# Later v loads, free accumulator banks for the first block's scores, and single vector steps per slot in an attention + FFN kernel

## The chip, the cores and the metric

The kernel runs on one core of a Trainium2 chip. The metric is the device time of one execution in microseconds, smaller being better. The core has TensorE (PE; its weight loads are listed apart as PEld), VectorE (DVE), ScalarE (ACT), GpSimd (POOL) and SyncE (SP, which here only issues transfers). Each engine takes its instructions in program order.

## What is computed

For each of 4 batches, with a sequence of 3136, `d_model` 256, `d_qk` 64 and `d_ff` 1024:

```python
scores = (1.0 / S) * z @ z.T                 # S x S, symmetric
attn   = np.maximum(scores, 0.0) ** 2
x      = u * (attn @ v)
h      = np.maximum(x @ w_in, 0.0)
conv   = sum(conv_w[k] * shift(h, k - 1) for k in range(3))   # along the sequence
out    = (h / (1 + np.exp(-conv))) @ w_out
```

## The kernel before

**Tiles.** The sequence of a batch is cut into 7 blocks of 448 columns; 28 blocks in all. For each block the kernel walks over 25 row tiles of 128 rows; one row tile of one block is a *slot*, so there are 700 slots. To keep float32 accuracy every operand of a product is split into a high and a low part (`vh`/`vl`, `ah`/`al`, `gh`/`gl`, ...) and a product is three matmuls.

**Attention.** For a computed row tile `k`, `scores` runs two matmuls into an accumulator bank with the tag `s` (two such banks), `relu` (ACT) writes the scaled ReLU to SBUF tile `t`, `square` (DVE, L309) multiplies in place in the bank, `split_hi` (ACT, `ah`) and `split_lo` (DVE, `al`, recorded at the helper's L122) make the two parts, and `attend` runs six matmuls (L337 to L339) into the two `av` banks. `split_lo` is the last reader of the `s` bank. Because the scores are symmetric, a part of the row tiles of a block is not computed: `part` (GpSimd, L270) copies `t` to a tile `pl` (three buffers), `spill` (SP, L282) writes it to a scratch tensor `dq`, and a later block takes it back with `fetch` (SP, a transposing transfer, L290), `join` (GpSimd, L296, tile `tj`) and a Square on ACT (L301). In block q of a batch 0, 3, 7, 10, 14, 17 and 21 of the 25 row tiles come back that way.

**FFN.** The FFN of block b runs during the slots of block b+1, in eight steps f of 128 columns, which begin at the slots `FS`. `ffn_in` runs six matmuls (L370 to L372, twice) into a bank with the tag `ph` (two banks); ReLU to `hb` (ACT, L393), first tap (ACT, L402, in place in `ph`), two more taps (DVE, L407), Sigmoid (ACT, L414), the product with `hb` (DVE, L421), then `gh` (ACT) and `gl` (low part, L122), and ten slots after `ffn_in` the products `ffn_out` (L438 to L440). For blocks q of 0 to 2 the low part is on GpSimd: then the product goes to an SBUF tile `c` and the `ph` bank is free after it. For q of 3 to 6 it is on DVE: the product stays in the `ph` bank, which is free after `gl`.

**v.** `load_v` (SP, L168) brings two row tiles of v into a tile `vst` (three buffers); `prep_v` copies them to `vh` (ACT) and makes `vl` (GpSimd, L122). In block 0 this runs just ahead of the use; for the next batches it runs in the last block of the batch before and in the first of its own.

**Order.** The order is written by hand. In slot k the engines receive: class PRE; `split_hi`, `split_lo` of row tile k+2; class MID; `relu`, `square` of k+3; class VEC; class POST; `fetch` of k+9, `join` of k+5, `part` of k+2, `spill` of k+1; class PE0; `attend` of k; `scores` of k+4; class PE1. The FFN's steps are put into these classes by `at(slot, class, ...)`. The number after `C_` is the class (0 PRE to 5 PE1), the other constants are slots after the step's first one.

Of the kernel before, what the change touches and what calls it, by code (L numbers as in the profile page):

```python
# [8 lines left out]
F32 = mybir.dt.float32  # L9
# [19 lines left out]
LA, LT, LS = 4, 3, 2  # L29
# [1 line left out]


FS = [2, 5, 8, 11, 15, 18, 21, 24]
RELU, TAP, ST1, ST2, SIG, GATE, GHI, GLO, OUT0, OUT1 = 1, 1, 2, 2, 3, 4, 5, 6, 10, 11
EVAC = 12
XS = 1

C_GATE, C_ST1, C_ST2, C_G, C_SIG, C_HI, C_LO = 0, 2, 2, 2, 3, 3, 2
C_TAP, C_XS, C_EV, C_V = 3, 3, 3, 5

QV = 3


WS = [0, 8, 11, 17, 15, 21, 27, 22, 29, 34, 36, 38, 40, 45, 48, 53]
# [14 lines left out]
def kernel(  # L59
# [15 lines left out]
    P = 128  # L75
    NB = 448
    QB = S // NB
    NJ = (S + P - 1) // P
# [11 lines left out]
    ps = ctx.enter_context(tc.tile_pool(name="ps", bufs=1, space=bass.MemoryType.PSUM))  # L90
# [14 lines left out]
    def at_slot(k):  # L105
        blk, i = divmod(k, NJ)
        return blk, *ent[blk % QB][i]
# [139 lines left out]
    def scores(k):  # L247
        blk, j, tr = at_slot(k)
        if tr:
            return  # L250
        s = ps.tile([P, 512], F32, tag="s", name="s", bufs=2)
        w = slice(j * P, (j + 1) * P)
        nc.tensor.matmul(s[:, :NB], lhsT=zhh[:, w], rhs=zq[blk], start=True, stop=False)  # L253
        nc.tensor.matmul(s[:, :NB], lhsT=zll[:, w], rhs=zq[blk], start=False, stop=True)  # L254
        sc[k] = s
# [108 lines left out]
    ph, hb, cc, gg, po = {}, {}, {}, {}, {}  # L364
# [30 lines left out]
            nc.gpsimd.tensor_copy(halo[:, f], t[:, NB : NB + 2])  # L395

    def ffn_tap(blk, f):
        e = width(blk)  # L400
        cc[blk, f] = c = ph.pop((blk, f))[:, :e]
        nc.scalar.mul(c, hb[blk, f][:, :e], cw[:, f, 0:1])  # L402
# [68 lines left out]
    V, A, G = nc.vector, nc.scalar, nc.gpsimd  # L471
# [4 lines left out]
    PRE, MID, VEC, POST, PE0, PE1 = range(6)  # L476

    def at(slot, cls, fn, *args):
        ev[slot][cls].append((fn, args))


    for q in range(2, QB):
        s = (7 * q) // 2 - LA - 2
# [1 line left out]
        at(s, POST, prep_z, q)  # L485
    at(-3, POST, prep_z, 1)
    for j in range(2, NJ, 2):
        at(max(j - 9, -LA), POST, load_v, 0, j)
        at(j - 3, C_V, prep_v, j, A)


    for b in range(1, B):
        k0 = (b * QB - 1) * NJ
        for q in range(QB):
            s = k0 - (QB - 2 - q) * NJ + (12 if q % 2 == 0 else 4)
            if q == QB - 2:
                s = k0 + 6
            elif q == QB - 1:
                s = k0 + NJ + 6
            at(s - 4, POST, load_z, b, q)  # L500
            at(s, POST, prep_z, q)
        last = {j: i for i, (j, _) in enumerate(ent[QB - 1])}
        for j in range(0, NJ, 2):
            s = k0 + max(last[j] + 2, last.get(j + 1, 0) + 2, V0 + V1 * j // NJ)
            at(s - 6, POST, load_v, b, j)
            at(s, C_V, prep_v, j, A)
    for blk in range(1, NBLK):
        at(blk * NJ - LA - 2, VEC, queries, blk)
# [2 lines left out]
    for i, (_, what, f) in enumerate(sorted(need)):  # L511
        s = WS[i]
# [8 lines left out]
    for blk in range(NBLK - 1):  # L521
        k0 = (blk + 1) * NJ
        at(k0, C_GATE, gate_x, blk, G)
        at(k0 + XS, C_XS, split_x, blk, (G, G))
        for f in range(FC):
            s = k0 + FS[f]
            at(s, POST, ffn_halo, blk, f)
            at(s, PE1, ffn_in, blk, f)
            at(s + RELU, C_TAP, ffn_relu, blk, f)
            at(s + TAP, C_TAP, ffn_tap, blk, f)  # L530
            at(s + ST1, C_ST1, ffn_conv, blk, f, 1)
            at(s + ST2, C_ST2, ffn_conv, blk, f, 2)
            at(s + SIG, C_SIG, ffn_sig, blk, f)
            lo = V if (blk + 1) % QB >= QV else G
            at(s + GATE, C_G, ffn_gate, blk, f, lo)
            at(s + GHI, C_HI, ffn_hi, blk, f, A)
            at(s + (GLO if lo is V else GHI), C_LO if lo is V else PE1, ffn_lo, blk, f, lo)
            at(s + OUT0, PE0, ffn_out, blk, f, 0)
            at(s + OUT1, PE0, ffn_out, blk, f, 1)
        at(s + EVAC, C_EV, evac, blk)  # L540
        at(s + EVAC + 2, POST, store, blk)
# [28 lines left out]
    with tc.manual_schedule():  # L570
# [12 lines left out]
        for k in range(-LA, max(ev) + 1):  # L583
            e = ev[k]
            run(e[PRE])
            if 0 <= k + LS < NS:
                split_hi(k + LS)
                split_lo(k + LS)
            run(e[MID])
            if 0 <= k + LT < NS:  # L590
                relu(k + LT)
                square(k + LT)
            run(e[VEC])
            run(e[POST])
            if 0 <= k + LD < NS:
                fetch(k + LD)
            if 0 <= k + LJ < NS:
                join(k + LJ)
            if 0 <= k + LP < NS:
                part(k + LP)  # L600
            if 0 <= k + LX < NS:
                spill(k + LX)
            run(e[PE0])
            if 0 <= k < NS:
                attend(k)
            if k + LA < NS:
                scores(k + LA)
            run(e[PE1])
# [41 lines left out]
```

## Time and profile before

| | us |
|---|---|
| median of 3 runs | 1699.93 (1699.38 to 1700.0) |
| the profiled execution | 1699.81 |
| its span, first to last instruction | 1697.7 |
| mean granted TensorE clock | 0.992 |

The profiled execution lies 2.1 us above its span and 0.1 us below the median of the runs. Matmuls are pipelined: each is recorded with about 0.37 us, while in a stretch without stalls one starts every 0.2 us or so. The busy share of TensorE therefore hides short stalls, and the number of matmuls in a stretch, against its length, says more.

### The profile page before, as it was taken

The numbers are of one execution on the slowest core, as the hardware profiler recorded it, in microseconds if no ns is written. First come the engines' busy times: TensorE is split into PE (matmuls) and PEld (weight loads), VectorE is DVE, ScalarE is ACT, GpSimd is POOL, SyncE is SP. The second block draws the span as 40 slices with busy tenths as digits, with TensorE's granted clock in tenths as the row PEclk, the third lists the DMA queues.
The fourth block names the chain that finished last, engine by engine and source line by source line (L and its number), as shares of the span: only waits on it lengthen the run. The fifth ranks groups of instructions, "written<-read, shape, count | busy, mean of one in ns | idle before, by whom it ended". The sixth has DMA issues, their size and how long they took to land.

```text
span 1697.7 us, 24837 instructions
## 1 busy us (share of the span) xinstructions
PE 1615.3 (95%) x7656; PEld 1433.9 (84%) x7656; DVE 1215.1 (72%) x2080; ACT 1277.1 (75%) x2562; POOL 982.5 (58%) x1345
## 2 busy tenths in 40 slices
PE   6689999999999999999999999999999999999998
PEld 5578888888889888888888988889889898888886
DVE  5788667776777767677767766777677776677766
ACT  5577777778777777777887777777877777777785
POOL 5767555556566654546575665555657566445551
PEclk9899999999999999999999999999999999999999
DMA  5543444456324434445543343454634334444540
GB/s 154 154 116 103 111 108 90 106 119 148 107 88 125 109 87 123 99 108 112 124 140 84 107 120 98 102 108 106 133 100 139 93 92 107 103 104 98 109 93 22
DMA packets 384485, 184.59 MB, mean 109 GB/s; under 512 B 275296, under 2 KB 383328, under 8 KB 384352
## 3 DMA queue, kind: packets, MB, share of 16 engines
q1 hardware_dynamic: 384208, 182.77, 43.5%
q8 instruction: 60, 0.98, 0.2%
q14 instruction: 73, 0.60, 0.1%
q10 hardware_dynamic: 144, 0.23, 0.0%
HBM read 36.59 MB, written 80.28 MB: 69 GB/s over the span
## 4 chain that ended last, share of the span: by engine, by line
PE 72%; DVE 13%; issue 6%; ACT 6%; POOL 1%; DMA 1%; SPq 0%; POOLq 0%; DVEq 0%; ACTq 0%
PE av L337 11%; PE av L338 11%; PE av L339 11%; PE ph L370 6%; PE ph L372 5%; PE ph L371 5%; PE s L253 5%; PE o L440 4%; PE o L438 4%; PE o L439 4%; PE s L254 4%; DVE al L122 3%; DVE s L309 3%; DVE ph L407 3%; ACT t L304 2%
## 5 line engine op out<-in xcount | busy, mean ns | idle before, releaser
L122 DVE TENSOR_TENSOR al<-s,ah 128x448 fp32r<-128x448 f32 x672 | 418.1, 622 | 369.1 <-ACT ah L316 198.4
L337 PE MATMUL av<-ah,vl 128*128 128x448 f32 x1344 | 496.0, 369 | 10.2 <-POOL vl L122 7.8
L338 PE MATMUL av<-ah,vh 128*128 128x448 f32 x1344 | 494.6, 368 | 0.0
L339 PE MATMUL av<-al,vh 128*128 128x448 f32 x1344 | 493.1, 367 | 0.0
L296 POOL COPY tj<-tp 128x896 uint16<-128x896 uint16 x288 | 348.4, 1214 | 1.9 <-DMA tp<-dq 1.5
L304 ACT ACTIVATE t<-s 128x448 f32<-128x448 f32 x412 | 225.4, 547 | 129.9 <-PE s L254 104.7
L407 DVE SCALAR_TENSOR_TENSOR ph<-hb,cw,ph 128x448 f32<-128x448 f32 (+1 forms) x448 | 306.8, 685 | 13.1 <-ACT ph L402 5.4
L309 DVE TENSOR_TENSOR s<-s,t 128x448 f32<-128x448 f32 x412 | 258.7, 628 | 78.2 <-ACT t L304 77.2
L270 POOL COPY pl<-t 128x896 uint16<-128x896 uint16 x312 | 290.7, 940 | 14.8 <-DMA dq<-pl 13.8
L395 POOL COPY halo<-hb 128x2 f32<-128x2 f32 x192 | 37.0, 192 | 451.1 <-ACT hb L393 450.7
L316 ACT CAST ah<-s 128x448 fp32r<-128x448 f32 x412 | 219.2, 532 | 98.0 <-DVE s L309 97.0
L337 PEld LDWEIGHTS av<-ah,vl 128*128 128x128 f32 x1344 | 254.6, 189 | 36.4 <-POOL vl L122 10.4
L339 PEld LDWEIGHTS av<-al,vh 128*128 128x128 f32 x1344 | 254.4, 189 | 21.3
L338 PEld LDWEIGHTS av<-ah,vh 128*128 128x128 f32 x1344 | 254.8, 190 | 20.4
L393 ACT ACTIVATE hb<-ph 128x448 f32<-128x448 f32 x224 | 122.6, 547 | 118.8 <-PE ph L372 117.2
L253 PE MATMUL s<-zq,zhh 128*128 128x448 f32 x412 | 163.6, 397 | 39.8 <-DVE al L122 31.0
L370 PE MATMUL ph<-xh,wih 128*128 128x448 f32 x448 | 171.9, 384 | 28.1 <-DVE gl L122 26.0
L314 ACT ACTIVATE ah<-tj 128x448 fp32r<-128x448 f32 x288 | 165.1, 573 | 0.0
L372 PE MATMUL ph<-xl,wih 128*128 128x448 f32 x448 | 164.8, 368 | 0.0
L438 PE MATMUL o<-gh,wol 128*128 128x448 f32 (+1 forms) x448 | 164.7, 368 | 0.0
L440 PE MATMUL o<-gl,woh 128*128 128x448 f32 (+1 forms) x448 | 164.1, 366 | 0.6 <-POOL gl L122 0.6
L371 PE MATMUL ph<-xh,wil 128*128 128x448 f32 x448 | 164.5, 367 | 0.0
(79 smaller groups left out, 2418.3 us busy)
## 6 DMA issues: line engine op xcount, KB each, us to landing
dq<-pl SPq DMA_DIRECT2D x252, 224.0 KB, 2.3
ut<-in_u_dram SPq DMA_DIRECT2D x28, 448.0 KB, 4.1
vst<-in_v_dram SPq DMA_DIRECT2D x48, 256.0 KB, 2.9
dq<-pl SPq DMA_DIRECT2D x84, 112.0 KB, 2.4
out_dram<-ob SPq DMA_DIRECT2D x20, 448.0 KB, 3.3
zt<-in_z_dram SPq DMA_DIRECT2D x28, 224.0 KB, 3.2
tp<-dq SPq DMA_TRANSPOSE x288, 3.3
wr<-in_moe_w_in_dram SPq DMA_DIRECT2D x8, 256.0 KB, 3.6
```

Of the source, the lines that this page charges most:

```text
L122: eng.tensor_tensor(out=out, in0=a, in1=b.bitcast(F32), op=ALU.subtract)
L270: nc.gpsimd.tensor_copy(pl[k], rl.pop(k).bitcast(U16).rearrange("p (n h) -> p h n", h=2))
L296: nc.gpsimd.tensor_copy(tj[k].bitcast(U16).rearrange("p (n h) -> p h n", h=2), t)
L304: nc.scalar.activation(rl[k], sc[k][:, :NB], AF.Relu, scale=SC1)
L309: nc.vector.tensor_tensor(out=s, in0=s, in1=rl[k], op=ALU.mult)
L337: nc.tensor.matmul(o, lhsT=vl[:, j, d], rhs=h, start=first, stop=False)
L338: nc.tensor.matmul(o, lhsT=vh[:, j, d], rhs=h, start=False, stop=False)
L339: nc.tensor.matmul(o, lhsT=vh[:, j, d], rhs=l, start=False, stop=False)
L370: nc.tensor.matmul(o, lhsT=wih[:, dc, w], rhs=xh[blk][:, dc], start=(dc == 0), stop=False)
L371: nc.tensor.matmul(o, lhsT=wil[:, dc, w], rhs=xh[blk][:, dc], start=False, stop=False)
L372: nc.tensor.matmul(o, lhsT=wih[:, dc, w], rhs=xl[blk][:, dc], start=False, stop=(dc == DC - 1))
L407: nc.vector.scalar_tensor_tensor(out=c, in0=hb[blk, f][:, k : e + k], scalar=cw[:, f, k : k + 1], in1=c, op0=ALU.mult, op1=ALU.add,)
```

## The change

- `load_v` moves: in block 0 from slot j-9, class POST, to slot j-7, class PE1; for the other batches from six slots ahead of `prep_v`, POST, to five slots ahead, PE1. In a slot, PE1 stands behind `fetch` and `spill`.
- The scores of the odd row tiles of block 0 go to the `ph` banks, so that block 0 has four banks for its scores.
- The low part of the gate is on GpSimd in every block but the last one's own FFN.
- The first tap moves from POST of slot 1 to MID of slot 2, the third tap from VEC of slot 2 to VEC of slot 3, and the Sigmoid from POST of slot 3 to MID of slot 4. The product stays in VEC of slot 4, `gh` in POST of slot 5, `gl` of GpSimd in PE1 of slot 5.

```diff
-RELU, TAP, ST1, ST2, SIG, GATE, GHI, GLO, OUT0, OUT1 = 1, 1, 2, 2, 3, 4, 5, 6, 10, 11
+RELU, TAP, ST1, ST2, SIG, GATE, GHI, OUT0, OUT1 = 1, 2, 2, 3, 4, 4, 5, 10, 11
-C_GATE, C_ST1, C_ST2, C_G, C_SIG, C_HI, C_LO = 0, 2, 2, 2, 3, 3, 2
-C_TAP, C_XS, C_EV, C_V = 3, 3, 3, 5
-QV = 3
+C_GATE, C_ST1, C_ST2, C_G, C_SIG, C_HI = 0, 2, 2, 2, 1, 3
+C_RELU, C_TAP, C_XS, C_EV, C_V = 3, 1, 3, 3, 5
...
-        s = ps.tile([P, 512], F32, tag="s", name="s", bufs=2)
+        tag = "ph" if k < NJ and k % 2 else "s"
+        s = ps.tile([P, 512], F32, tag=tag, name="s", bufs=2)
...
-        at(max(j - 9, -LA), POST, load_v, 0, j)
+        at(max(j - 7, -LA), PE1, load_v, 0, j)
...
-            at(s - 6, POST, load_v, b, j)
+            at(s - 5, PE1, load_v, b, j)
...
-            at(s + RELU, C_TAP, ffn_relu, blk, f)
+            at(s + RELU, C_RELU, ffn_relu, blk, f)
...
-            lo = V if (blk + 1) % QB >= QV else G
-            at(s + GATE, C_G, ffn_gate, blk, f, lo)
+            at(s + GATE, C_G, ffn_gate, blk, f, G)
...
-            at(s + (GLO if lo is V else GHI), C_LO if lo is V else PE1, ffn_lo, blk, f, lo)
+            at(s + GHI, PE1, ffn_lo, blk, f, G)
```

## Rows read from the trace of the kernel before

**Rows 1.** The page, busy time: us, share of the span, instructions.
```profile
PE 1615.3 (95%) x7656; PEld 1433.9 (84%) x7656; DVE 1215.1 (72%) x2080; ACT 1277.1 (75%) x2562; POOL 982.5 (58%) x1345
```

**Rows 2.** Windows, one per block: length, busy us (instructions) of PE, PEld, DVE, ACT, POOL; clock.
```profile
11.50:84.10 72.60, 53.98 (x198) 41.98 (x196) 51.27 (x86) 40.66 (x88) 52.30 (x56) 0.88 0.52 152
84.10:150.40 66.30, 58.75 (x267) 51.45 (x266) 56.30 (x105) 49.29 (x107) 45.82 (x63) 0.95 0.44 120
...
501.60:560.50 58.90, 58.77 (x288) 53.36 (x286) 42.26 (x73) 43.75 (x88) 35.24 (x49) 1.00 0.40 112
...
619.90:680.20 60.30, 56.92 (x273) 50.59 (x272) 42.47 (x73) 44.19 (x89) 31.14 (x44) 1.00 0.42 105
680.20:738.30 58.10, 56.05 (x267) 49.24 (x267) 41.39 (x71) 43.80 (x89) 30.96 (x43) 1.00 0.49 104
738.30:792.80 54.50, 53.33 (x259) 48.16 (x259) 39.37 (x68) 43.67 (x89) 30.78 (x42) 1.00 0.51 107
792.80:848.50 55.70, 54.59 (x261) 48.21 (x261) 39.40 (x68) 46.10 (x94) 31.80 (x41) 1.00 0.53 122
```

**Rows 3.** Waits of TensorE from 150 to 1660 us: total us, times, longest.
```profile
PE ph L370 <- DVE gl L122: 22.3, 33, 1.2
PE s L253 <- DVE al L122: 13.8, 19, 1.1
```

**Rows 4.** Waits of ScalarE over the whole span: total us, times, longest.
```profile
ACT hb L393 <- PE ph L372: 117.2, 187, 1.5
ACT t L304 <- PE s L254: 104.7, 204, 1.8
```

**Rows 5.** Timelines of TensorE and VectorE in slot 11 of block 10.
```profile
646.28 0.36 PE L339 MATMUL av<-al,vh 128*128 128x448 f32 x1
647.40 0.47 PE L370 MATMUL ph<-xh,wih 128*128 128x448 f32 x1 [0.77 <-DVE gl L122]
...
646.74 0.61 DVE L122 TENSOR_TENSOR gl<-ph,gh 128x448 fp32r<-128x448 f32 x1
```

**Rows 6.** Waits of SyncE's queue: total us, times, longest.
```profile
SPq L168 <- POOL vl L122: 63.6, 18, 7.0
```

**Rows 7.** The chain that ended last, in block 0: start us, us, what.
```profile
28.67 1.28 POOL vl L122
29.97 0.37 SPq L168
...
30.38 3.20 DMA dq<-pl
...
34.59 1.28 POOL vl L122
```

**Rows 8.** Waits of TensorE from 84 to 150 us.
```profile
PE s L253 <- DVE al L122: 5.1, 4, 2.3
```

**Rows 9.** Groups by line and shape: count, busy us, mean ns of one, idle before.
```profile
L407 DVE SCALAR_TENSOR_TENSOR ph<-hb,cw,ph 128x448 f32<-128x448 f32 x384 | 262.9, 685 | 8.3 <-ACT ph L402 1.5
...
L402 ACT ACTIVATE ph<-hb,cw 128x448 f32<-128x448 f32 x192 | 122.7, 639 | 16.8
L414 ACT ACTIVATE ph<-ph 128x448 f32<-128x448 f32 x192 | 102.4, 533 | 32.3 <-DVE ph L407 32.2
...
L122 DVE TENSOR_TENSOR gl<-ph,gh 128x448 fp32r<-128x448 f32 x128 | 78.6, 614 | 0.0
...
L122 POOL TENSOR_TENSOR gl<-c,gh 128x448 fp32r<-128x448 f32 x64 | 74.6, 1166 | 21.2 <-ACT gh L125 20.7
```

**Rows 10.** Timelines of GpSimd and ScalarE: a join in block 13, its Square.
```profile
797.96 1.22 POOL L296 COPY tj<-tp 128x896 uint16<-128x896 uint16 x1
...
800.96 0.55 ACT L301 ACTIVATE s<-tj 128x448 f32<-128x448 f32 x1
```

**Rows 11.** Timeline of block 10: a low part on GpSimd, VectorE beside it.
```profile
625.46 1.16 POOL L122 TENSOR_TENSOR gl<-c,gh 128x448 fp32r<-128x448 f32 x1
...
626.10 0.63 DVE L309 TENSOR_TENSOR s<-s,t 128x448 f32<-128x448 f32 x1
```

**Rows 12.** The page, transfers: count, KB each, median us from issue to landing.
```profile
vst<-in_v_dram SPq DMA_DIRECT2D x48, 256.0 KB, 2.9
```

## The prediction

> **What bounds the kernel now.** I read the page first, then the windows of each block, then the waits, and last the timeline around single stalls. TensorE is busy 95% of the span and no other engine over 75% [rows 1]; but a busy TensorE hides stalls, so the windows matter more. Block 8, where the low part of the gate is already on GpSimd, starts 288 matmuls in 58.9 us, one every 0.2045 us [rows 2]. I take that as the pace without stalls. At it, blocks 10 to 13 (the blocks q of 3 to 6, where the low part is on DVE) would need 55.8, 54.6, 53.0 and 53.4 us for their 273, 267, 259 and 261 matmuls; they take 60.3, 58.1, 54.5 and 55.7 [rows 2]. That is 4.5, 3.5, 1.5 and 2.3 us of stalls, 11.8 a batch. Block 0 needs 198 x 0.2045 = 40.5 us and takes 72.6, block 1 needs 54.6 and takes 66.3 [rows 2]. So there are three places to gain: block 0, block 1, and the small stalls of the later blocks.
>
> In the later blocks TensorE waits for two things: `ffn_in` for a `ph` bank that `gl` on DVE has not given back (22.3 us, 33 times), and `scores` for an `s` bank that `al` has not given back (13.8 us, 19 times) [rows 3]. The waits count less than the stall costs: in slot 11 of block 10 two matmuls start 1.12 us apart where 0.2045 is the pace, a loss of 0.92, and the row gives 0.77 [rows 5]. So 0.15 is added to each wait. ScalarE is not the one that holds back: it waits for TensorE itself, 187 times for `ffn_in` and 204 times for the scores [rows 4]. A stall of TensorE that goes is thus time won, until these waits are used up.
>
> In block 0 the chain runs in a circle of two slots. SP's queue stands at `load_v` until `vl` on GpSimd gives a `vst` buffer back: 63.6 us in 18 waits [rows 6]. The load goes out at 29.97, 0.02 us after `vl` of 28.67 ends; only behind it, at 30.38, goes the spill of `pl`, which takes 3.20 us to land; GpSimd's next `part` needs that buffer, and its next `vl` starts at 34.59 [rows 7]. The circle is 5.92 us for two slots, which over 25 slots makes 74 us, about what the block takes.
>
> **The change, part by part.**
>
> *The low part of the gate.* 128 steps of 614 ns leave DVE (79 us) and come to GpSimd at 1166 ns (149 us) [rows 9]. Off DVE they also leave the `ph` bank: it is free after the product in VEC of slot 4 instead of after `gl` in VEC of slot 6. The next user of the bank is two steps, six or seven slots, on, in PE1. The margin grows from under one slot to two slots, over 4 us at 54.5 us for 25 slots [rows 2], and the longest wait is 1.2 us [rows 3]. I take all of these waits as gone: 22.3 + 33 x 0.15 = 27 us. From below it could be 15, if half come back as waits of the next kind.
>
> GpSimd pays 8 x 1.17 = 9.3 us a block, on top of 31 to 32 us in blocks of 54 to 60 [rows 2, 9]; it is not the bound. The low part is queued in front of the next `join`. In the tightest case that I found in block 13 the join ends at 799.18 and its Square starts at 800.96: a margin of 1.78 us, more than 1.17 [rows 10]. What covers it is that margin; without it, see the rivals. `ffn_out` reads `gl` five slots later. I cost it at nothing.
>
> Does a GpSimd step slow DVE? From 625.46 to 626.62 a low part runs on GpSimd and DVE's square beside it, at 626.10, takes 0.63 us [rows 11], no longer than others. The Trainium skill speaks against such a move in "Perfetto Trace Analysis", § Optimizing Scalar/DVE Operations: the two engines share an SBUF port, so handing work from one to the other may not help. In "SBUF — State Buffer", § Who interferes with whom, it says which VectorE steps that concerns: those with two SBUF inputs or in a two-port mode. By the first sentence the move would gain nothing or lose; by the second, and by the row, the steps here with their one input in PSUM go on undisturbed, and the sum stands.
>
> *Single vector steps.* Before, both DVE taps stand in one slot: 2 x 685 ns between the square of one row tile and `al` of the next [rows 9]. Now one stands there and the other a slot later, so `al` behind the pair comes about 0.69 us earlier. The waits of `scores` for `al` are 13.8 + 19 x 0.15 = 16.7 us [rows 3]; one wait is 0.73 us on average and costs 0.88 (longest 1.1). A cut of 0.69 takes most of each; some are longer. I take two thirds, 11 us; the bounds are 0 and 16.7. Against that, the tap (639 ns) and the Sigmoid (533 ns) [rows 9] now stand in MID ahead of `relu`, the first link of the scores' chain. `relu` waits for the scores anyway in 204 slots, 104.7 us, 0.51 on average [rows 4], so most of it is covered; no instruction is added. The Sigmoid waits for the second DVE tap of the slot before, with `relu` queued behind it on ScalarE; that tap is set right behind the square that `ah`, ahead of the Sigmoid, needs too, so I add nothing. At a block's start a Sigmoid now stands ahead of `xh`, for which `ffn_in` waits: 0.533 x 27 = 14 us at most, taken as nothing, as `ffn_in` is two slots away. What is late next if the cover is missing is `square`, `ah`, `al` and the bank: see the rivals.
>
> *Loads of v later, four banks in block 0.* A load of slot j-7, PE1, finds the buffer given back in slot j-9, and stands behind the slot's spill and fetch, so the circle is cut. What is next: GpSimd is busy 52.3 us in the block and DVE 51.3 [rows 2]; block 0 can't be shorter than that, a gain of at most 20.3 us. The most loaded engine beside TensorE elsewhere is DVE in block 1, 56.3 of 66.3 us, 85% [rows 2]; at 85% GpSimd's 52.3 make 61.5 us. I take 61.5, a gain of 11 us; the bounds are 0 and 20. The four banks give `scores` two slots more, so that DVE's bursts of weight preparation don't stop TensorE; without them DVE would be what replaces the circle, and I add nothing for them. For later batches the load still has five slots, 10.9 us at 54.5 for 25, for a landing of 2.9 [rows 2, 12]: nothing lost or won.
>
> *Block 1.* DVE is busy 85% of it. TensorE waits 5.1 us in 4 waits for `al` [rows 8]; each shorter by one tap of 0.685 is 2.7, I take 3 (0 to 5.1 + 4 x 0.15 = 5.7).
>
> *Sum*: 27 + 11 + 11 + 3 = 52 us off the profiled execution's 1699.81 (span 1697.7 and 2.1 around it), which is 0.1 below the median: **1648 us**. All upper bounds together, 27 + 16.7 + 20.3 + 5.7 = 70, give 1630; the lower ones, 15 + 0 + 0 + 0, give 1685. The clock should stay at 1.00 in the blocks where it is, and rise in block 0 from 0.88 [rows 2] as TensorE stalls less.
>
> **The rivals.**
> - *Block 0 stays.* GpSimd and DVE are both busy about 70% there, and their turns may take the circle's place. Then 11 us are missing: 1659. Against it: the rows name a landing of 3.20 us in each circle in which neither of them works.
> - *The scores' chain gets longer.* Tap and Sigmoid ahead of `relu` cost 0.639 - 0.51 and 0.533 - 0.51 for each of 27 x 8 = 216 steps, 0.15 x 216 = 32 us, and the 11 us of `al` don't come: 1648 + 43 = 1691. Against it: the waits of ScalarE for TensorE are 222 us in all [rows 4].
> - *GpSimd is late with joins* (the other side). It is in order, waits for `gh`, then does `gl`, and the join behind it comes after its Square is due. If each of the 128 cost TensorE the 1.17 less the 0.51 that ScalarE waits anyway, 84 us are added: 1732. It decides from 52 / 128 = 0.41 us a step on. Against it: the margin of 1.78 us [rows 10] and 60% load.
> - *DVE is held during GpSimd's step.* If DVE loses 1166 ns for each step and saves 614, 0.55 x 128 = 71 us come onto DVE; on the path, and with the 27 us of the banks lost, 1648 + 71 + 27 = 1746. Against it: the 0.63 us above [rows 11]. This is the shared port of "Perfetto Trace Analysis", as the Trainium skill has it.
> - *Nearly everything goes*: 1625 to 1632, by the upper bounds.
>
> **How the numbers follow.** Chances: the forecast 0.57 (its own range 1632 to 1664), block 0 stays 0.15, longer chain 0.13, late joins 0.05, DVE held 0.03, everything goes 0.07. The range from 1624 to 1690 leaves out the two slow cases, half of the longer chain and a little below, under 2 in 10. A change under 0.2% (3.4 us) can't be told from none here. Slower is 0.08, the two slow cases; 0.03 of the longer chain ends near 1700 and counts as the same; faster 0.89.
>
> **What would show it.** In the profile after: the wait of `ph` for `gl` is gone; `al` waits of `scores` are fewer and shorter; blocks 10 to 13 come to about 56, 55, 53.5 and 54 us; DVE's busy time falls by some 79 us and GpSimd's rises by some 149; SP no longer waits for `vl` at L168, and block 0 takes about 61 us. Wrong would be: new waits of ScalarE for `tj`, longer DVE rows beside GpSimd, more `al` waits, or a block 0 that still takes over 70 us with another engine in the chain.

## The result and the profile after

The changed kernel takes 1624.32 us (median of 4 runs, 1623.78 to 1625.38) against 1699.97 (1699.38 to 1701.4): a ratio of 0.9555, 95% interval 0.9538 to 0.9571, or 75.7 us less. The forecast was 1648, in a range of 1624 to 1690. The result lies 23.7 us under the forecast, 0.3 us inside the low end of the range and just under the rival "nearly everything goes" (1625 to 1632). The profiled execution took 1625.38 with a span of 1623.4.

The page of the kernel after, busy time as in [rows 1]:

```profile
PE 1585.0 (98%) x7656; PEld 1441.2 (89%) x7656; DVE 1161.0 (72%) x1952; ACT 1262.5 (78%) x2562; POOL 1125.4 (69%) x1473
```

Windows of the kernel after, one per block, columns as in [rows 2]: blocks 0 and 1, block 2, then blocks 10 to 13, and last the tail behind the last `attend`:

```profile
9.10:71.50 62.40, 49.46 (x197) 41.23 (x196) 54.98 (x89) 41.59 (x91) 51.96 (x56) 0.86 0.61 181
71.50:136.00 64.50, 56.02 (x266) 49.01 (x266) 58.98 (x105) 49.34 (x108) 46.52 (x64) 0.99 0.46 123
136.00:197.20 61.20, 60.06 (x281) 54.74 (x282) 44.76 (x76) 44.68 (x93) 39.65 (x54) 0.95 0.37 99
590.50:646.30 55.80, 55.73 (x274) 50.87 (x272) 38.77 (x66) 42.90 (x88) 37.96 (x50) 1.00 0.47 111
646.30:700.90 54.60, 54.55 (x268) 49.89 (x268) 37.28 (x64) 43.93 (x90) 39.72 (x52) 1.00 0.49 109
700.90:753.60 52.70, 52.54 (x259) 48.33 (x258) 35.13 (x60) 42.80 (x88) 38.20 (x50) 1.00 0.53 110
753.60:807.50 53.90, 53.41 (x261) 48.68 (x261) 36.49 (x61) 46.13 (x95) 42.71 (x51) 1.00 0.58 131
1589.60:1623.40 33.80, 28.12 (x131) 23.72 (x129) 23.30 (x39) 21.68 (x42) 8.91 (x25) 1.00 0.07 28
```

Set against the blocks of before, the 74.3 us between the two spans come from here:

| stretch | before | after | |
|---|---|---|---|
| up to the first `attend` | 11.5 | 9.1 | -2.4 |
| block 0 | 72.6 | 62.4 | -10.2 |
| block 1 | 66.3 | 64.5 | -1.8 |
| block 2 | 60.5 | 61.2 | +0.7 |
| blocks 3 to 27 | 1449.9 | 1392.4 | -57.5 |
| tail | 36.9 | 33.8 | -3.1 |

Blocks 3 to 27 as one stretch, before and then after, columns as in [rows 2]:

```profile
210.90:1660.80 1449.90, 1410.94 (x6779) 1260.80 (x6778) 1033.64 (x1765) 1113.02 (x2225) 833.37 (x1145) 1.00 0.45 108
197.20:1589.60 1392.40, 1387.73 (x6779) 1270.14 (x6778) 975.81 (x1639) 1100.72 (x2224) 974.72 (x1270) 1.00 0.47 112
```

Block 2 stands at a granted clock of 0.95 after, 1.00 before. From 134.9 to 141.7 us the kernel after runs at the lower of the clock's two levels (1.2 and 2.4 GHz), and its matmuls start 0.373 us apart there. So the +0.7 of this block can't be told from the cost of the clock.

Blocks 10 to 13 lost 4.5, 3.5, 1.8 and 1.8 us. The stalls that the prediction read out of the pace there were 4.5, 3.5, 1.5 and 2.3: these blocks now run at the pace, and 77% of the gain lies in blocks 3 to 27. All waits of TensorE from 140 to 1586 us in the kernel after, columns as in [rows 3]:

```profile
PE s L253 <- DVE al L120: 4.9, 13, 0.6
```

The wait of `ph` for `gl` is gone, and of `al`'s 13.8 us a third is left. Whether ScalarE holds TensorE back now, its waits after tell, columns as in [rows 4]:

```profile
ACT ah L316 <- DVE s L309: 136.0, 248, 2.9
ACT t L304 <- PE s L254: 107.5, 174, 2.6
ACT hb L393 <- PE ph L372: 49.8, 119, 1.3
...
ACT s L301 <- POOL tj L296: 0.5, 1, 0.5
```

ScalarE waits 67 us less for `ffn_in` than before, 39 us more for DVE's square (97.0 before), and still has 157 us of waits for TensorE in the second and third row: it is not the bound. The last row is the only wait for a join in the whole span; before there was one as well, of 1.2 us.

### The profile page after: what moved, and what is told of

It reads as the page before. It is cut to its first block, busy times and chain, and to the rows that moved or that the text cites. A ratio compares the mean times of both kernels' runs of the same rounds, so it can differ in the third digit from the quotient of the medians.

```text
span 1623.4 us, 24961 instructions
## 1 busy us (share of the span) xinstructions
PE 1585.0 (98%) x7656; PEld 1441.2 (89%) x7656; DVE 1161.0 (72%) x1952; ACT 1262.5 (78%) x2562; POOL 1125.4 (69%) x1473
## 4 chain that ended last, share of the span: by engine, by line
PE 86%; ACT 5%; DVE 4%; issue 3%; POOL 1%; DMA 1%; POOLq 0%; SPq 0%; ACTq 0%; DVEq 0%
PE av L337 15%; PE av L338 15%; PE av L339 15%; PE ph L370 5%; PE ph L372 5%; PE o L439 5%; PE ph L371 5%; PE o L437 5%; PE s L253 5%; PE o L438 5%; PE s L254 5%; DVE al L120 1%; ACT t L304 1%; DVE ph L406 1%; ACT xh L360 1%
## 5 line engine op out<-in xcount | busy, mean ns | idle before, releaser
L120 POOL TENSOR_TENSOR gl<-c,gh 128x448 fp32r<-128x448 f32 (+1 forms) x220 | 256.2, 1165 | 59.9 <-ACT gh L123 57.4
L337 PEld LDWEIGHTS av<-ah,vl 128*128 128x128 f32 x1344 | 254.2, 189 | 40.8 <-POOL vl L120 12.3
L253 PE MATMUL s<-zq,zhh 128*128 128x448 f32 x412 | 157.5, 382 | 18.7 <-DVE al L120 9.5
L370 PE MATMUL ph<-xh,wih 128*128 128x448 f32 x448 | 164.4, 367 | 1.1 <-DVE c L420 0.6
L438 PE MATMUL o<-gh,woh 128*128 128x448 f32 (+1 forms) x448 | 164.2, 366 | 0.0
```

Source lines behind the costliest of these rows:

```text
L120: eng.tensor_tensor(out=out, in0=a, in1=b.bitcast(F32), op=ALU.subtract)
L337: nc.tensor.matmul(o, lhsT=vl[:, j, d], rhs=h, start=first, stop=False)
L370: nc.tensor.matmul(o, lhsT=wih[:, dc, w], rhs=xh[blk][:, dc], start=(dc == 0), stop=False)
L438: nc.tensor.matmul(o, lhsT=woh[:, f, d], rhs=h, start=False, stop=False)
```

## The experiments

The kernel before was timed again beside each experiment; its medians were 1698 to 1700. Unless it is said otherwise, an edit is made to the kernel before and the gain is worked out from the ratio. First the change taken apart: the loads and banks, and the two halves of the FFN's part.

**Loads of v and the banks, without the FFN's part.**

```diff
-        s = ps.tile([P, 512], F32, tag="s", name="s", bufs=2)
+        tag = "ph" if k < NJ and k % 2 else "s"
+        s = ps.tile([P, 512], F32, tag=tag, name="s", bufs=2)
...
-        at(max(j - 9, -LA), POST, load_v, 0, j)
+        at(max(j - 7, -LA), PE1, load_v, 0, j)
...
-            at(s - 6, POST, load_v, b, j)
+            at(s - 5, PE1, load_v, b, j)
```

> The kernel before with the later v loads and the four score banks of block 0 alone. If the parts are independent: the lead-in, block 0 and block 1 get shorter by what the changed kernel shows there, 2.4 + 10.2 + up to 1.8 us, and the later blocks stay at 60.3, 58.1, 54.5 and 55.7 us: 1700 - 13 = 1687 (1684 to 1690). If the later blocks gained from the loads being later as well: under 1675. If block 0 only gained because less DVE work followed it: over 1695.

Measured 1685.04 us, ratio 0.9924 (0.9909 to 0.9939), about 13 us less. Blocks 3 to 27 take 1449.3 us, as before. What this part brings is brought at the start of the span.

**The low part of the gate on GpSimd, in the old slots.**

```diff
-QV = 3
+QV = 7
```

> The kernel before with the low part of the gate on GpSimd in all blocks, the FFN's steps in their old slots. Theory 1, the stalls of the later blocks are the ph bank held until gl, and the s bank held behind the pair of DVE taps: the waits for gl go, those for al stay or grow a little, 1700 - 27 to 35 = 1665 to 1673. Theory 2, the single steps do the work and the bank is secondary: 1690 or more. Theory 3, GpSimd is late with joins when its low part waits for gh: slower than 1700.

Measured 1656.84, ratio 0.9754 (0.9739 to 0.9768), about 42 us less where term A of the prediction had 27.

**The single steps, with the low part left where it was.**

```diff
-RELU, TAP, ST1, ST2, SIG, GATE, GHI, GLO, OUT0, OUT1 = 1, 1, 2, 2, 3, 4, 5, 6, 10, 11
+RELU, TAP, ST1, ST2, SIG, GATE, GHI, GLO, OUT0, OUT1 = 1, 2, 2, 3, 4, 4, 5, 6, 10, 11
-C_GATE, C_ST1, C_ST2, C_G, C_SIG, C_HI, C_LO = 0, 2, 2, 2, 3, 3, 2
-C_TAP, C_XS, C_EV, C_V = 3, 3, 3, 5
+C_GATE, C_ST1, C_ST2, C_G, C_SIG, C_HI, C_LO = 0, 2, 2, 2, 1, 3, 2
+C_RELU, C_TAP, C_XS, C_EV, C_V = 3, 1, 3, 3, 5
...
-            at(s + RELU, C_TAP, ffn_relu, blk, f)
+            at(s + RELU, C_RELU, ffn_relu, blk, f)
```

> The kernel before with the moved first tap, third tap and Sigmoid alone; the low part on DVE as before in the blocks q of 3 to 6. Theory 1: waits of scores for al mostly go, waits of ffn_in for gl stay, 1700 - 15 to 25 = 1675 to 1685. Theory 2 (the single steps do it): 1650 or less. The rival of the longer chain (tap and Sigmoid ahead of relu): 1705 or more.

Measured 1664.92, ratio 0.98 (0.9785 to 0.9814), about 34 us less: more than the 15 to 25 of theory 1, and less than the 50 of theory 2. TensorE's waits from 145 to 1620 us in this kernel:

```profile
PE ph L370 <- DVE gl L122: 14.9, 27, 1.0
PE av L337 <- DVE ut L348: 3.6, 1, 3.6
PE s L253 <- DVE al L122: 2.8, 5, 0.8
```

With the pair of taps parted, not only the waits for `al` shrink, those for `gl` on DVE do too. The two FFN edits thus act in part on the same stalls.

**Both halves of the FFN's part**, the two diffs above together:

> The kernel before with the low part on GpSimd and the single steps, without the later loads and the four banks. If the parts add up: what the changed kernel shows from block 2 on and in the tail, 57 + 3 us, 1700 - 60 = 1640 (1636 to 1644), block 0 still 72 us. If block 0's stall is hidden behind something else once the rest is faster, or the loads help the later blocks too: further off, over 1645.

Measured 1636.21, ratio 0.9631 (0.9615 to 0.9647), 62.6 us less, where the halves alone make 42 + 34 = 76. Some 13 us are reached by either. With the loads and banks (13) it makes 76, and the whole change measured 75.7: the start and the FFN's part add up.

**What of the start is the loads', and what the banks'.** The first diff above was cut in two, its last two edits alone and its first edit alone.

> The kernel before with the later v loads alone; block 0 keeps two banks for its scores. The two parts together gave 13.8 us. If the circle of SP's queue, spill, pl and vl is what held block 0, the loads give most of it: 8 to 13 us, 1686 to 1692, and scores then wait for al behind DVE's weight preparation. If the banks were the cause: 0 to 3 us, over 1696.

> The kernel before with the four score banks of block 0 alone, v loads as before. If the circle holds block 0, two more banks let TensorE run ahead and wait elsewhere: 0 to 3 us, 1696 to 1700, the waits of scores for al gone and those of attend for vl longer. If the banks were the cause: 8 us or more, under 1691.

The loads alone: 1687.48, ratio 0.9933 (0.9919 to 0.9948), 11 us less. The banks alone: 1697.64, ratio 0.9994 (0.9985 to 1.0004), no change. Block 0 of the kernel with loads and banks, then with the loads alone, then with the banks alone, columns as in [rows 2]:

```profile
8.70:71.40 62.70, 48.95 (x198) 39.66 (x196) 56.26 (x90) 41.75 (x92) 52.61 (x56) 0.89 0.60 180
```
```profile
11.30:71.50 60.20, 47.37 (x198) 36.85 (x196) 53.58 (x87) 40.31 (x89) 52.15 (x56) 0.97 0.61 179
```
```profile
8.90:82.00 73.10, 49.24 (x197) 40.38 (x196) 52.07 (x90) 42.49 (x92) 52.80 (x56) 0.91 0.52 152
```

The banks let the first `attend` begin 2.5 us earlier, but block 0 ends at 71.4 or 71.5 either way; it is the loads that move its end from 84.1. TensorE's waits up to 75 us tell what holds it then. With the loads alone and with the banks alone they begin with:

```profile
PE s L253 <- DVE al L122: 13.7, 14, 2.1
```
```profile
PE av L338 <- POOL vl L122: 19.2, 9, 3.5
```

With the banks alone, `attend` waits for `vl`, whose load still stands in the circle of [rows 7]. With the loads alone it is `scores` that waits, for a bank that `al` on DVE has not given back. Whether the banks add the 2 us between 1685.04 with them and 1687.48 without can't be told: the intervals overlap.

**Is it DVE's load, or the bank?** The product goes to the SBUF tile `c` in every block but the last, while the low part stays on DVE:

```diff
-        if lo is nc.gpsimd:
+        if lo is nc.gpsimd or blk < NBLK - 1:
```

> The kernel before with one line changed: in every block the product of the gate goes to the SBUF tile c, so that the ph bank is free after it, but the low part stays on DVE in the blocks q of 3 to 6, so that DVE's work is the same. The low part on GpSimd in all blocks gave 42 us. If that came from the bank being free earlier: the waits of ffn_in for gl go here too, 1699 - 30 to 42 = 1657 to 1669. If it came from DVE having 79 us less to do: under 12 us, over 1687. With both: between.

Measured 1663.99, ratio 0.9794 (0.978 to 0.9809), 35 us less with the same number of steps on every engine. That is 35 of the 42 us of the move to GpSimd: it is the bank given back early that pays. The steps are the same in number but not in time: the low part now reads `c` and `gh`, both in SBUF, and takes 828 ns on DVE on average instead of 614, 27 us more in all (see the last section). Whether these make the 7 us between 35 and 42 is not shown. TensorE no longer waits for `gl` at all in this kernel; from 145 to 1620 us its waits begin with:

```profile
PE s L253 <- DVE al L122: 17.0, 23, 1.2
```

**Which of the single steps it is.** Three edits to the changed kernel. In the first only the third tap is late, the first tap and the Sigmoid are back in POST of slots 1 and 3. In the second the third tap is back beside the second in slot 2. In the third only the first tap is back.

```diff
-RELU, TAP, ST1, ST2, SIG, GATE, GHI, OUT0, OUT1 = 1, 2, 2, 3, 4, 4, 5, 10, 11
+RELU, TAP, ST1, ST2, SIG, GATE, GHI, OUT0, OUT1 = 1, 1, 2, 3, 3, 4, 5, 10, 11
-C_GATE, C_ST1, C_ST2, C_G, C_SIG, C_HI = 0, 2, 2, 2, 1, 3
-C_RELU, C_TAP, C_XS, C_EV, C_V = 3, 1, 3, 3, 5
+C_GATE, C_ST1, C_ST2, C_G, C_SIG, C_HI = 0, 2, 2, 2, 3, 3
+C_RELU, C_TAP, C_XS, C_EV, C_V = 3, 3, 3, 3, 5
```

> The changed kernel with the first tap and the Sigmoid back in POST (of slots 1 and 3), the third tap staying one slot after the second. If setting the two DVE taps apart is what takes the waits of scores for al away: 1624, within 3 us. If the first tap and the Sigmoid in MID matter (they come out of the stretch between relu and the next ah on ScalarE): 1630 to 1645, with more al waits. If they cost something by standing ahead of relu: under 1621.

Measured 1654.34, ratio 0.9736 (0.972 to 0.9752): 30 us slower than the changed kernel. The miss shows a link between two of the moves. ScalarE from 150 to 1620 us in this kernel, and one slot of it on DVE and on ScalarE:

```profile
ACT ph L413 <- DVE ph L406: 205.1, 191, 2.2
```
```profile
618.77 0.63 DVE L309 TENSOR_TENSOR s<-s,t 128x448 f32<-128x448 f32 x1 [0.58 <-ACT t L304]
619.31 0.68 DVE L406 SCALAR_TENSOR_TENSOR ph<-hb,cw,ph 128x448 f32<-128x448 f32 x1
621.03 0.62 DVE L120 TENSOR_TENSOR al<-s,ah 128x448 fp32r<-128x448 f32 x1 [1.05 <-ACT ah L316]
```
```profile
620.02 0.53 ACT L413 ACTIVATE ph<-ph 128x448 f32<-128x448 f32 x1 [1.29 <-DVE ph L406]
620.46 0.54 ACT L316 CAST ah<-s 128x448 fp32r<-128x448 f32 x1
```

The square ends at 619.40, and `ah` could start. But in program order the Sigmoid of the same slot stands ahead of it and waits for the tap until 619.99; `ah` starts at 620.46 and `al` at 621.03, 1.63 us behind the square. The same place in the changed kernel, DVE and then ScalarE:

```profile
608.98 0.63 DVE L309 TENSOR_TENSOR s<-s,t 128x448 f32<-128x448 f32 x1 [0.86 <-ACT t L304]
609.52 0.68 DVE L406 SCALAR_TENSOR_TENSOR ph<-hb,cw,ph 128x448 f32<-128x448 f32 x1
610.22 0.62 DVE L120 TENSOR_TENSOR al<-s,ah 128x448 fp32r<-128x448 f32 x1
```
```profile
609.65 0.54 ACT L316 CAST ah<-s 128x448 fp32r<-128x448 f32 x1 [0.70 <-DVE s L309]
610.24 0.53 ACT L413 ACTIVATE ph<-ph 128x448 f32<-128x448 f32 x1
```

Here `ah` goes first, and `al` starts 0.61 us behind the square's end. Whoever parts the taps must move the Sigmoid too.

```diff
-RELU, TAP, ST1, ST2, SIG, GATE, GHI, OUT0, OUT1 = 1, 2, 2, 3, 4, 4, 5, 10, 11
+RELU, TAP, ST1, ST2, SIG, GATE, GHI, OUT0, OUT1 = 1, 2, 2, 2, 4, 4, 5, 10, 11
```

> The changed kernel with the third tap back beside the second in slot 2; the first tap and the Sigmoid stay in MID of slots 2 and 4. With all three steps in their old slots and the rest changed the sum of the runs so far gives 1656.8 - 13.8 = 1643; the changed kernel has 1624.3. The prediction's step (the pair of taps on DVE holds al back): most of the 19 us are lost, 1637 to 1643. If it is the first tap and the Sigmoid, moved out of the stretch of ScalarE between relu and the next ah: 1624 to 1629.

Measured 1645.93, ratio 0.9683 (0.9669 to 0.9696): 21.6 us slower than the changed kernel, 3 us beyond the range that the prediction's step had. TensorE's waits from 140 to 1580 us begin with:

```profile
PE s L253 <- DVE al L120: 12.1, 18, 1.6
```

The row of the changed kernel says 4.9. Of the 21.6 us some 17 lie in blocks 2 to 27, which these rows cover (1470.3 us against 1453.6), and 4.5 in block 1. So 7.2 us of recorded waits stand for some 17 us of time: the view of waits falls short by more than half here.

```diff
-RELU, TAP, ST1, ST2, SIG, GATE, GHI, OUT0, OUT1 = 1, 2, 2, 3, 4, 4, 5, 10, 11
+RELU, TAP, ST1, ST2, SIG, GATE, GHI, OUT0, OUT1 = 1, 1, 2, 3, 4, 4, 5, 10, 11
-C_RELU, C_TAP, C_XS, C_EV, C_V = 3, 1, 3, 3, 5
+C_RELU, C_TAP, C_XS, C_EV, C_V = 3, 3, 3, 3, 5
```

> The changed kernel with the first tap back in POST of slot 1; the third tap and the Sigmoid stay moved. The prediction's step: unchanged, 1624 to 1627. If the first tap behind ReLU holds the next ah back (0.64 us on ScalarE in 216 steps, more than the chain has to spare in some of them): 1630 to 1640. If the tap ahead of relu costs something: under 1622.

Measured 1625.0, ratio 0.9565 (0.9552 to 0.9578), the time of the changed kernel. Where the first tap stands makes no difference that can be told, so a tap ahead of `relu` has no cost that can be told either. So the 30 us of the first edit hang on the Sigmoid in its old place.

**What bounds block 0 now.** Two edits to the changed kernel. In the first, half of the squares of blocks 0 and 1 go from DVE to ScalarE. In the second, four of the low parts of v in block 0 go from GpSimd to DVE as well.

```diff
-            nc.vector.tensor_tensor(out=s, in0=s, in1=rl[k], op=ALU.mult)
+            if k < 2 * NJ and k % 2:
+                nc.scalar.activation(s, rl[k], AF.Square, scale=SC1**-0.5)
+            else:
+                nc.vector.tensor_tensor(out=s, in0=s, in1=rl[k], op=ALU.mult)
```

> The changed kernel, and the squares of the odd computed row tiles of blocks 0 and 1 on ScalarE instead of DVE. In the changed kernel DVE is busy 55.0 of 62.4 us in block 0 and 59.0 of 64.5 in block 1, ScalarE 41.6 and 49.3. If DVE's load bounds these blocks: some 24 squares of 0.54 us leave it, 3 to 8 us are won, 1616 to 1621. If GpSimd (52.0 us) is the one that bounds block 0: 0 to 3 us. If the extra step of ScalarE delays the next ah: slower, up to 1630.

```diff
-    def prep_v(j, eng, n=None):
+    def prep_v(j, eng, lo=nc.gpsimd):
...
-        sub(nc.gpsimd, vl[:, j : j + n], t[:, :n], vh[:, j : j + n])
+        sub(lo, vl[:, j : j + n], t[:, :n], vh[:, j : j + n])
...
-        at(j - 3, C_V, prep_v, j, A)
+        at(j - 3, C_V, prep_v, j, A, V if j % 6 == 4 else G)
```

> The kernel with the squares of the odd computed row tiles of blocks 0 and 1 on ScalarE (1623.4), and the low part of v of 4 of block 0's 12 later pairs (4, 10, 16, 22) on DVE instead of GpSimd. There TensorE still waited 11.2 us for vl of GpSimd, with DVE relieved. If GpSimd is what bounds block 0 now: 4 x 1.3 = 5.2 us leave it, 3 to 5 us are won, 1618 to 1621, the waits for vl shorter. If the queue's order and not the load makes vl late, or the two engines hold each other up: 0 to 1 us, 1622 to 1625.

Measured 1623.44, ratio 0.9556 (0.9543 to 0.957), and 1621.41, ratio 0.9546 (0.9533 to 0.9559). Block 0 of the two:

```profile
9.10:69.80 60.70, 46.92 (x198) 39.40 (x197) 50.06 (x76) 47.78 (x104) 52.06 (x55) 0.92 0.63 186
```
```profile
8.90:67.40 58.50, 48.39 (x198) 40.47 (x197) 50.35 (x80) 47.16 (x103) 47.90 (x51) 0.91 0.66 192
```

Neither edit makes the kernel faster by what can be told: both intervals overlap the changed kernel's, and 1621.41 lies between the two ranges expected for it. For the block alone there is a measure of the noise. Its code is the same in the changed kernel, in the one with loads and banks alone and in the three edits of the single steps, and there it takes 62.4, 62.7, 62.7, 61.9 and 61.1 us. Taking 5 us from DVE leaves 60.7, hardly below these. Taking 4 us from GpSimd on top leaves 58.5, 2.6 below the lowest, and TensorE's waits for `vl` of GpSimd up to 137 us fall from 11.2 to 6.3, with 1.6 for those now on DVE. That the block follows GpSimd rather than DVE is thus what one profile of each kernel suggests. In block 1 the first edit takes 5.5 us from DVE, and the block does not get shorter than its 64.5:

```profile
69.80:135.10 65.30, 57.29 (x267) 50.56 (x265) 53.48 (x96) 54.06 (x119) 46.85 (x66) 0.97 0.45 122
```

The chain that ended last, in block 0 of the changed kernel, start and length in us:

```profile
44.88 1.24 POOL vl L120
46.11 0.19 issue
46.34 0.74 POOL wil L120
47.08 0.87 POOL pl L270
47.96 1.16 POOL zll L120
...
50.42 1.41 POOL vl L120
51.87 0.47 PE av L337
```

GpSimd works with hardly a gap and `attend` waits for its `vl`. Before, a landing stood in this place [rows 7].

## Why the prediction came out so

**What bounds the kernel: right for the later blocks and block 0.** TensorE's stalls in the later blocks and the circle in block 0 were the two large places, and time won there stayed won. DVE's load in block 1 was not shown to be a bound: 5.5 us less of it did not shorten the block. The prediction read the 63.6 us in 18 waits of [rows 6] as those of block 0; they are those of the whole span. Up to 85 us the row is:

```profile
SPq L168 <- POOL vl L122: 34.3, 9, 6.1
```

The circle itself, 5.92 us for two slots [rows 7], stands. The pace of one matmul every 0.2045 us held: blocks 10 to 13 came to 55.8, 54.6, 52.7 and 53.9 where about 56, 55, 53.5 and 54 were forecast.

**The step that failed is the size of terms A and B.** The prediction had two readings of the same stalls and took the smaller. The windows gave 11.8 us for the four later blocks of a batch, 47 in all. The waits gave, for all batches, 22.3 + 13.8 us in 52 waits plus 0.15 each, 43.9 at most, and 27 + 11 were taken. Measured were 62.6 for the two together; by the table above 57.5 of the whole change lie in blocks 3 to 27: 46 in the blocks q of 3 to 6, and 12 in those of q 0 to 2, where the prediction had looked at block 8 alone, which gained 0.2 (its neighbours 7 and 9 gained 2.0 and 1.6).

Why the waits fall short shows in the starts of the matmuls before. A matmul is recorded with 0.36 us while one starts every 0.2045, so a late start of up to some 0.16 us leaves no idle time between two recorded matmuls, and no wait. And behind the stall of [rows 5] the next matmul comes late as well:

```profile
647.72 0.36 PE L371 MATMUL ph<-xh,wil 128*128 128x448 f32 x1
```

It starts 0.32 us after the one at 647.40, not 0.2045: another 0.115 that the 0.15 didn't hold. All 6781 matmuls of blocks 3 to 27 can be read this way. The median distance between two starts is 0.203 us in every kernel below; the table sums what the distances exceed it by, for the matmuls of `ffn_in` and of `scores`, in us.

| kernel | `ffn_in` | `scores` | blocks 3 to 27 shorter by |
|---|---|---|---|
| before | 41.2 | 30.0 | |
| low part on GpSimd | 0.0 | 31.0 | 40.3 |
| product in `c` | 0.1 | 33.2 | 33.5 |
| single steps | 30.4 | 9.6 | 31.1 |
| both halves | 0.3 | 12.3 | 58.1 |
| changed kernel | 0.4 | 12.3 | 57.5 |

So the stalls behind the two rows of [rows 3] were 71 us, not 43.9. The two halves overlap because the single steps alone take 11 us from `ffn_in` as well, which the low part on GpSimd takes whole.

*Term A* (27, bounds 15 to 27): the low part on GpSimd alone gave 42, and 35 of them came with the bank alone. The mechanism was right: all late starts of `ffn_in` went. They were 41 us, so the upper bound was not one.

*Term B* (11, bounds 0 to 16.7): 21 us beside A (62.6 less 42), 34 by itself. The third tap brought it, as foretold, but only together with the Sigmoid. The share of two thirds nearly held, 17.7 of 30.0 us; the price of the whole, 16.7, was too low. The sentence that the Sigmoid costs nothing, since the tap that it waits for is "set right behind the square", was right for its place in MID; in POST of the third tap's slot it cost 30 us.

That the result lies inside the range is luck in part. The end of the range, 1624, lies 6 us below what all upper bounds together gave, and no term of the sum stands behind these 6.

**Term C** (11; block 0 at 61.5) measured 62.4, with another 2.4 from the earlier first `attend`; loads and banks alone made 13, the loads alone 11. "I add nothing" for the banks stands. That GpSimd would be the next, about 85% busy, came near: 51.96 of 62.40 us, 83%. The 85% were borrowed from another engine in another block, so the close fit is partly luck, and DVE is busier than GpSimd there, 54.98 us. SP's wait for `vl` is not gone, as the list of signs had it, but in the first 75 us it is down to two, and the queue's largest row there is now the spill's wait for GpSimd's `part`:

```profile
SPq L282 <- POOL pl L270: 28.3, 16, 4.0
SPq L166 <- POOL vl L120: 3.9, 2, 3.2
```

**Term D** (3) measured 1.8 in block 1. The single steps, from which it was to come, brought some 0.7 of these: with them but without the loads and banks, block 1 takes 65.6 us where it took 66.3.

**Not foreseen:** the tail, 3.1 us shorter. It takes 36.9 and 36.6 us in the kernels before and with the loads alone, where its granted clock is 0.95; 35.8 at 1.00 with the loads and banks; and 33.8 at 1.00 with both halves of the FFN's part and no more. So about 1 us goes with the clock and 2 with the FFN's part.

**Signs that were wrong.** The granted clock in block 0 did not rise from 0.88; it is 0.86, a mean between the levels of 1.2 and 2.4 GHz. With the loads alone it is 0.97, yet the block ends at the same 71.5. DVE's busy time fell by 54 us, not 79, GpSimd's rose by 143 (149 forecast). DVE's steps overlap in the record when they follow each other: in the slot of the changed kernel above a step of 0.63 us starts 0.54 before the next. Without the 128 steps DVE's busy time before is 65 us lower, not 79. And DVE's steps that prepare the weights and copy `zq` grew from 64.5 to 76.8 us (the last section has such a step). That makes 53 of the 54.

**The rivals.** *Block 0 stays* and *the longer chain* did not come: block 0 fell by 10, and moving the first tap out of `relu`'s way changed nothing. *Late joins* stayed away, but the cover is nearly used up. Block 13's tightest case after, GpSimd and then ScalarE:

```profile
768.20 1.22 POOL L296 COPY tj<-tp 128x896 uint16<-128x896 uint16 x1
```
```profile
769.68 0.53 ACT L301 ACTIVATE s<-tj 128x448 f32<-128x448 f32 x1
```

The join ends at 769.42, the Square that reads it starts at 769.68: a margin of 0.26. Matched one by one, in the order of the slots, 34 of 288 joins now end less than 0.5 us ahead of their Square, against six before. The 1.78 of [rows 10] was not the tightest case of that block: in the kernel before a join that begins at 812.97 ends 0.99 us ahead of its Square, less than the 1.17 of a low part. So the margin that the prediction named did not rule this rival out.

*DVE held* did not come in the FFN's and the scores' steps, only in the 12 us of steps on weights and `zq` above. By shape, mean ns of one, after:

```profile
L120 DVE TENSOR_TENSOR al<-s,ah 128x448 fp32r<-128x448 f32 x672 | 418.8, 623 | 232.4 <-ACT ah L314 162.1 <-ACT ah L316 57.1 <-PE av L338 2.4
L406 DVE SCALAR_TENSOR_TENSOR ph<-hb,cw,ph 128x448 f32<-128x448 f32 x384 | 261.6, 681 | 1.3 <-ACT ph L401 1.2
```

The tap took 685 before [rows 9] and takes 681 with 143 us more of GpSimd beside it.

## What to carry over

Where a pipelined TensorE is the bound, size its stalls by matmuls per stretch against the pace of a stretch without stalls; rows of waits find the cause but here held 36 of some 71 us. A bank whose content is copied out one step earlier can be worth more than taking the step itself off an engine. When one vector step is moved, look at what stands in order behind the step that waits for it on the other engine: two moves that gain together can lose 30 us when one is left out.

## What the runs showed of the hardware

VectorE's steps whose inputs all lie in SBUF can get longer beside GpSimd. The run with the product in `c` shows it best, as its low part on DVE reads two SBUF tiles where before it read one and the bank:

```profile
L122 DVE TENSOR_TENSOR gl<-c,gh 128x448 fp32r<-128x448 f32 x128 | 106.0, 828 | 0.0
```

Of these 128 steps the 73 that begin while no GpSimd step runs take 611 to 620 ns; the 55 that begin beside one take 1111 ns on average, up to 1499. In the kernel before, with one input in PSUM, the 54 that begin beside a GpSimd step take 611 to 616 ns.

The steps on weights show it too. DVE in block 0 of the changed kernel, start and length:

```profile
30.73 0.28 DVE L205 TENSOR_SCALAR wm<-wr 128x256 uint32<-128x256 uint32 x1
...
37.84 1.23 DVE L205 TENSOR_SCALAR wm<-wr 128x256 uint32<-128x256 uint32 x1
```

and GpSimd beside the second:

```profile
37.73 1.19 POOL L120 TENSOR_TENSOR zll<-zt,zhh 128x448 fp32r<-128x448 f32 x1
```

The same step takes 0.28 us or 1.23; its mean over 16 is 681 ns after, 506 before. Beside the first, too, a GpSimd step runs, but a short one that begins 0.03 us behind it. The Trainium skill has this in "SBUF — State Buffer", § Who interferes with whom, as a lock on ports that VectorE and GpSimd share, and the steps with two SBUF inputs agree with it, as do the steps with an input in PSUM, which kept their 681 and 623 ns. The step on weights has one SBUF input; which case of that rule it is, no run here shows.
